# Early weight pieces kept in one line each, the last output tiles stored in four parts from two queues, and a new order of loads and due times, in an attention kernel with two expert layers

## The chip, the cores and the metric

The kernel runs on one core of a Trainium2 chip. The time is device microseconds of one execution. PE is the matrix engine, with PEld for its weight loads; DVE is the vector engine, ACT the scalar engine, POOL GpSimd, and SP the engine that only issues DMAs. 16 DMA engines move the data of all queues.

## What is computed

Four batches of eight heads pass through an attention over 32 memory slots; the result goes through a leaky expert layer with weights `w_in` and `w_out`, and then through four experts that are mixed by `domain_probs`. The weights of the first layer arrive as float64 and are rebuilt as float32 on the chip.

```python
a = softmax(phi, axis=2)                       # over 576 positions
k_m, v_m = a.T @ k, a.T @ v                    # 32 slots per head
attn = softmax(scale * q @ k_m.T) @ v_m
x = attn.transpose(0, 2, 1, 3).reshape(2304, 512)
h = x @ w_in;  x = maximum(0.01 * h, h) @ w_out
p = domain_probs / domain_probs.sum(-1)
for e in range(4):
    out += p[:, e:e+1] * (maximum(x @ w1[e], 0) @ w2[e])
```

## The kernel before, in words

Every float32 product is made of three products of rounded parts (a high and a low part of each operand). Work runs in three stages: the attention of batch 0 with the first weight pieces; the first expert layer (lines L960 and L1027 to L1029), with the attention of batches 1 to 3 and further weight pieces placed between; and the second layer (L1136 and L1204 to L1206) with its output stores.

A planner (`Plan`) collects operations with an engine, an estimated cost and a due time, and `issue` writes them out in the order of its own clock. `SHIFTS` changes the due times of ranges of operations. What each engine does is therefore a fixed row; each engine works through its row in order, and an instruction that waits holds everything behind it on that engine.

The loads of `phi`, `k`, `q` and `v` of each batch, the raw weight pieces and the stores are all issued by SP. Eight DMA semaphores are used in turn, so a DMA also waits for the one eight places ahead of it to land.

A raw weight piece (512 KB, 1,024 numbers of 4 bytes on each partition) lands in one of three buffers (`raws`) or, for the fourth to the seventh piece, in room that is still free in `xx`, which later holds the first layer's sum (`more0` to `more3`). `xx` has four lines of 2,304 numbers on each partition, a line being split in four stretches of 576, one for each batch; the same room holds `k`, `v` and `q` of the batches until they are used (`HOME`: batch 1's `v` in stretch 1 of all four lines, its `q` in stretch 2, its `k` in stretch 3). Before the change a `more` piece lies in 512 columns of one stretch of two neighbouring lines. The distance between its first and its last number then spans parts of all stretches of these lines. The waits that the framework puts in go by such spans: in the program before, steps on `more` pieces wait for batch 1's `v` load, which touches none of their numbers, and that load waits for steps on `more` pieces.

`piece64` rebuilds a piece in four steps on ACT, DVE and POOL (L858, L862, L870 or L868, L878); `split` then makes the two rounded parts (L341, L344). Each token tile of the second layer's last group ends in one DVE operation (L1223), after which SP stores 128 rows of 2 KB (L1235); stores of earlier groups (L1231) are made in four parts of 32 rows.

Of the kernel before, what the change touches and what calls it, by code (L numbers as in the profile page):

```python
# [15 lines left out]
ALU = mybir.AluOpType  # L16
# [4 lines left out]
SHIFTS = [  # L21
    (411, 34, 3.8), (30, 16, -39.9), (40, 2, -21.2), (265, 1, -16.9), (266, 2, -2.6), (440, 3, -3.1), (77, 12, -10.1)
]
# [13 lines left out]
class Plan:  # L37
# [6 lines left out]
    SPARE = 0.5  # L44
    NEAR = 0.1
    BANKS = 8

# [52 lines left out]
    def issue(self):  # L100
        ops = self.ops
# [14 lines left out]
        while issued < len(ops):  # L116
            now = events[0][0]
            while events and events[0][0] <= now:
                _, n, what = heappop(events)
# [9 lines left out]
            for e, queue in [(e, q) for q in (ready, spare) for e in names]:  # L129
                skipped = []  # L130
                while free[e] <= now and queue[e]:
                    item = heappop(queue[e])
                    n = item[1]
# [40 lines left out]
                    for m in after[n]:  # L174
                        late = self.TRANSFER if e == "SP" else 0.0 if e in ops[m][0] else self.LATENCY
                        there[m] = max(there[m], now + us + late)
                        left[m] -= 1
                        if not left[m]:
                            heappush(events, (there[m], m, None))
# [5 lines left out]
def kernel(  # L185
# [13 lines left out]
    nc = tc.nc  # L199
# [137 lines left out]
    def engine(e):  # L337
        return {"DVE": nc.vector, "POOL": nc.gpsimd}[e]
# [436 lines left out]
    def raw_piece(src, due, after, alone=False):  # L775
# [5 lines left out]
        if RAWS <= n < RAWS + MORE:  # L781

            x = n - RAWS
            t, rk = places["X"][:, 2 + x // 2, x % 2 * 2:x % 2 * 2 + 2, 0:512], f"more{x}"
            if len(src.shape) == 2:
                src = src.rearrange("p (a b) -> p a b", a=2)
        else:
# [54 lines left out]
    def piece64(kind, n, sl, src, due, key, after):  # L842
# [31 lines left out]
        def add(e, out):  # L874
            cuts = [(slice(i, i + 1),) for i in range(2)] if e == "DVE" and rk[0] == "m" else [()]
            for cut in cuts:
                cut = (every, *cut)
                engine(e).tensor_tensor(out=out[cut], in0=fu[cut], in1=low[cut], op=ALU.add)  # L878
        plan.op("DVE", 0.42, due, lambda: nc.vector.tensor_single_scalar(fu, fu, 3, op=ALU.logical_shift_left),
# [307 lines left out]
    def second_products(t, n):  # L1187
# [4 lines left out]
        for i in range(2 * TPB):  # L1192
# [34 lines left out]
            if u == E - 1:  # L1227
                def fn(tt=tt, a_=a_, dst=dst):
                    if dst is None:
# [3 lines left out]
                        return  # L1233
                    for i, n, at in runs_of(tt):
                        nc.sync.dma_start(out=rows_of(out, at, n), in_=dst[i:i + n * M])  # L1235
                plan.op("SP", 0.8, due, fn, [("out", tt)], [])
        freed["v2"] += 1

# [13 lines left out]
    for x in range(MORE):  # L1252
        plan.ops[loaded["q1" if x < 2 else "k1"]][3].update({plan.writer[f"more{x}"], *plan.readers[f"more{x}"]})
    for first, count, shift in SHIFTS:
# [33 lines left out]
```

## Time and profile before

| | us |
|---|---|
| median of 3 runs (lowest, highest) | 1167.89 (1167.64, 1168.8) |
| the profiled execution's own time | 1166.8 |
| its span, from the first to the last instruction | 1164.8 |
| PE busy in the span | 1127.9 |
| DVE, ACT, POOL busy | 680.5, 442.6, 101.1 |
| busy PE in the first 100 us | 79.91 |
| last DVE operation ends | 1148.78 |

The span is 2.0 us shorter than the execution's own time, and the profiled execution is 1.1 us below the median. PE is busy nearly without a break between the first 70 us and 1148 us; the stretches ahead of that and behind it are where an engine other than PE sets the time. In the views, a line number such as L1223 is a line of the kernel.

### The profile page before, as it was taken

To read this page: it belongs to the slowest core of one execution; us is meant where nothing else is said; L and a number is where in the kernel's file an instruction comes from. 1 tells how busy PE (TensorE), PEld (TensorE's weight loads), DVE (VectorE), ACT (ScalarE), POOL (GpSimd) and SP (SyncE) were. 2 spreads that over 40 slices of the span, in tenths; PEclk is the share of its full clock that TensorE was granted. 3 is DMA by queue.
4 is the path that set the end of the run, shared out by engine and by line. 5 is a ranking of instruction groups with operands and counts; after the bars stand their busy time and mean duration, and the time that the engine had idled before them with its cause. 6 is when DMAs were issued, how large, how long until landed. Compare 5 with 4: busy or idle time off the path is not lost.

```text
span 1164.8 us, 18127 instructions
## 1 busy us (share of the span) xinstructions
PE 1127.9 (97%) x7414; PEld 1020.6 (88%) x7414; DVE 680.5 (58%) x1276; ACT 442.6 (38%) x895; POOL 101.1 (9%) x103
## 2 busy tenths in 40 slices
PE   6799999999999999999999999999999999999994
PEld 4479999999999999898998999999999999999993
DVE  5796576733346787767677654454566634454641
ACT  4565567743435544333324223222224213222220
POOL 2341125500000000000000000000000000000000
PEclk9799999999999999999999999999999999999997
DMA  9564013310000377534444644444444634444201
GB/s 335 172 216 129 30 38 120 116 37 1 2 19 32 118 267 261 189 146 184 180 178 145 217 152 156 163 163 163 148 157 134 210 139 163 163 163 158 94 11 54
DMA packets 54013, 160.84 MB, mean 138 GB/s; under 512 B 5803, under 2 KB 22187, under 8 KB 47787
## 3 DMA queue, kind: packets, MB, share of 16 engines
q1 hardware_dynamic: 49323, 100.97, 24.7%
q0 software_dynamic: 4608, 58.72, 14.3%
q8 instruction: 58, 0.95, 0.3%
q14 instruction: 24, 0.20, 0.0%
HBM read 125.60 MB, written 34.08 MB: 137 GB/s over the span
## 4 chain that ended last, share of the span: by engine, by line
PE 92%; DMA 3%; DVE 2%; ACT 0%; POOL 0%; issue 0%; SPq 0%; POOLq 0%; ACTq 0%
PE psum L1136 30%; PE psum L1205 11%; PE psum L1206 11%; PE psum L1204 11%; PE psum L960 8%; PE psum L1027 6%; PE psum L1028 5%; PE psum L1029 5%; DMA exact<-in_moe_w_out_dram 2%; PE psum L976 1%; DMA exact<-in_q_dram 1%; DVE rounded L344 1%; DMA exact<-in_v_dram 0%; DVE exact L545 0%; PE psum L573 0%
## 5 line engine op out<-in xcount | busy, mean ns | idle before, releaser
L1145 DVE TENSOR_TENSOR exact<-psum,exact 128x384 f32<-128x384 f32 x336 | 184.0, 556 | 271.9 <-PE psum L1136 270.1
L1152 ACT ACTIVATE rounded<-exact 128x384 fp32r<-128x384 f32 x192 | 100.8, 525 | 283.5 <-DVE exact L1145 281.8
L344 DVE TENSOR_TENSOR rounded<-exact,rounded 128x288 fp32r<-128x288 f32 (+2 forms) x224 | 123.3, 565 | 105.6 <-ACT rounded L341 104.5
L1206 PE MATMUL psum<-late,rounded 128*128 128x512 f32 x384 | 150.7, 392 | 0.0
L1205 PE MATMUL psum<-late,rounded 128*128 128x512 f32 x384 | 150.5, 392 | 0.0
L1204 PE MATMUL psum<-late,rounded 128*128 128x512 f32 x384 | 149.3, 389 | 0.0
L1136 PE MATMUL psum<-rounded 128*128 128x384 f32 x768 | 143.4, 336 | 0.0
L1136 PEld LDWEIGHTS psum<-rounded 128*128 128x128 f32 x768 | 135.0, 188 | 2.4 <-DVE exact L1145 0.3
L960 PE MATMUL psum<-rounded 128*128 128x288 f32 x768 | 124.5, 299 | 2.3 <-DVE rounded L344 2.3
L341 ACT CAST rounded<-exact 128x288 fp32r<-128x288 f32 (+4 forms) x239 | 114.7, 500 | 17.4 <-DMA exact<-in_moe_w_dram 3.5
L1027 PE MATMUL psum<-rounded 128*128 128x288 f32 x384 | 116.0, 302 | 4.0 <-ACT rounded L341 4.0
L960 PEld LDWEIGHTS psum<-rounded 128*128 128x128 f32 x768 | 109.3, 189 | 8.6 <-issue 4.0
L1028 PE MATMUL psum<-rounded 128*128 128x288 f32 x384 | 113.6, 296 | 1.4 <-DVE rounded L344 1.4
L1029 PE MATMUL psum<-rounded 128*128 128x288 f32 x384 | 113.5, 296 | 0.0
L1136 PE MATMUL psum<-late,rounded 128*128 128x384 f32 x576 | 109.7, 336 | 0.0
L1156 DVE SCALAR_TENSOR_TENSOR rounded<-exact,rounded 128x384 fp32r<-128x384 f32 x192 | 98.7, 550 | 13.0 <-ACT rounded L1152 13.0
L1136 PEld LDWEIGHTS psum<-late,rounded 128*128 128x128 f32 x576 | 102.0, 188 | 3.8
L1015 ACT ACTIVATE exact<-psum 128x288 f32<-128x288 f32 x128 | 52.5, 410 | 123.3 <-PE psum L960 117.3
L1167 ACT COPY exact<-psum 128x384 f32<-128x384 f32 x48 | 23.1, 481 | 198.1 <-PE psum L1136 196.8
L1206 PEld LDWEIGHTS psum<-late,rounded 128*128 128x128 f32 x384 | 72.0, 188 | 15.1
L1205 PEld LDWEIGHTS psum<-late,rounded 128*128 128x128 f32 x384 | 72.0, 188 | 13.4
L1204 PEld LDWEIGHTS psum<-late,rounded 128*128 128x128 f32 x384 | 72.1, 188 | 13.2
(113 smaller groups left out, 1677.9 us busy)
## 6 DMA issues: line engine op xcount, KB each, us to landing
rounded<-kept POOLq DMA_DIRECT2D x22, 1792.0 KB, 7.7
exact<-in_moe_w_dram SPq DMA_DIRECT2D x64, 512.0 KB
kept<-rounded SPq DMA_DIRECT2D x10, 1792.0 KB
w<-kept POOLq DMA_DIRECT2D x10, 1792.0 KB, 7.8
kept<-w SPq DMA_DIRECT2D x6, 1792.0 KB
exact<-in_moe_w_in_dram SPq DMA_DIRECT2D x16, 512.0 KB
exact<-in_moe_w_out_dram SPq DMA_DIRECT2D x16, 512.0 KB
exact<-in_k_dram SPq DMA_DIRECT2D x4, 1152.0 KB
```

The costliest lines, as they stand in the source:

```text
L341: nc.scalar.copy(out, in_) if e == "ACT" else engine(e).tensor_copy(out, in_)
L344: engine(e).tensor_tensor(out=out, in0=in0, in1=in1, op=ALU.subtract)
L960: nc.tensor.matmul(ps, lhsT=l, rhs=r, start=start and n == 0, stop=stop and n == len(seq) - 1)
L1027: nc.tensor.matmul(po, lhsT=w2l[:, ds_], rhs=th, start=first, stop=False)
L1028: nc.tensor.matmul(po, lhsT=w2h[:, ds_], rhs=tl, start=False, stop=False)
L1029: nc.tensor.matmul(po, lhsT=w2h[:, ds_], rhs=th, start=False, stop=last)
L1136: nc.tensor.matmul(ps[k][0:TB], lhsT=l, rhs=r, start=(i == 0), stop=(i == 5))
L1145: plan.op("DVE", dve2(TB), at[k], lambda: nc.vector.tensor_tensor(out=o, in0=ps[k][0:TB], in1=other, op=ALU.add), [ps[k], ok, from_], [key])
L1152: plan.op("ACT", act2(TB), at[k], lambda: nc.scalar.activation(out=th, in_=src, func=AF.Relu), [key, *h_from[hs[c, i]]], [keys[0]])
L1204: nc.tensor.matmul(po[0:DM], lhsT=tl, rhs=w2h[:, c], start=(p == 0 and c == 0), stop=False)
L1205: nc.tensor.matmul(po[0:DM], lhsT=th, rhs=w2l[:, c], start=False, stop=False)
L1206: nc.tensor.matmul(po[0:DM], lhsT=th, rhs=w2h[:, c], start=False, stop=(p == NP2 - 1 and c == 1))
```

## The change

The three parts: `more` pieces of one line each, the last tiles' stores in parts of 32 rows (two from SP, two from ACT), and a new order (a constant `SETTLE` in the planner, which counts an operation that waits for a load as ready 2.5 us later, and new `SHIFTS`). DVE adds of a `more` piece are no longer cut in two.

```diff
 SHIFTS = [
-    (411, 34, 3.8), (30, 16, -39.9), (40, 2, -21.2), (265, 1, -16.9), ...
+    (553, 34, 1.0), (417, 30, 3.4), (490, 3, -13.8), (250, 28, -6.7), ...
 ]
...
+    SETTLE = 2.5
...
                         late = self.TRANSFER if e == "SP" else 0.0 if e in ops[m][0] else self.LATENCY
+                        late += self.SETTLE * (e not in ("SP", "X") and "SP" in ops[m][0])
...
             x = n - RAWS
-            t, rk = places["X"][:, 2 + x // 2, x % 2 * 2:x % 2 * 2 + 2, 0:512], f"more{x}"
-            if len(src.shape) == 2:
-                src = src.rearrange("p (a b) -> p a b", a=2)
+            t, rk = xx[:, x, 2 * S:2 * S + size], f"more{x}"
+            if len(src.shape) == 3:
+                t = t.rearrange("p (a b) -> p a b", a=src.shape[1])
...
         def add(e, out):
-            cuts = [(slice(i, i + 1),) for i in range(2)] if e == "DVE" and rk[0] == "m" else [()]
-            for cut in cuts:
-                cut = (every, *cut)
-                engine(e).tensor_tensor(out=out[cut], in0=fu[cut], in1=low[cut], op=ALU.add)
+            engine(e).tensor_tensor(out=out, in0=fu, in1=low, op=ALU.add)
...
-                    for i, n, at in runs_of(tt):
-                        nc.sync.dma_start(out=rows_of(out, at, n), in_=dst[i:i + n * M])
+                    for i in range(0, P // 2, M):
+                        nc.sync.dma_start(out=rows_of(out, tt * P + i)[0], in_=dst[i:i + M])
                 plan.op("SP", 0.8, due, fn, [("out", tt)], [])
+                if final:
+                    def fn(tt=tt, dst=dst):
+                        for i in range(P // 2, P, M):
+                            nc.scalar.dma_start(out=rows_of(out, tt * P + i)[0], in_=dst[i:i + M])
+                    plan.op("ACT", 0.8, due, fn, [("out", tt)], [])
...
     for x in range(MORE):
-        plan.ops[loaded["q1" if x < 2 else "k1"]][3].update({plan.writer[f"more{x}"], *plan.readers[f"more{x}"]})
+        for name in ("q1", "k1"):
+            plan.ops[loaded[name]][3].update({plan.writer[f"more{x}"], *plan.readers[f"more{x}"]})
```

SP's row from its eighth load on, before. `att<-in_q` is batch 2's `q`, `exact<-in_v` and `exact<-in_q` are batch 1's `v` and `q`; names in brackets are the engines, or the earlier DMAs (DMAHW), that a row waits for.

```order
L523 DMA att<-in_q_dram 128x4x576 [waits DMAHW4_49,DMAHW0_49,PE_49]
L160 DMA exact<-in_moe_w_in_dram 128x2x512 [waits DMAHW1_49]
L160 DMA exact<-in_moe_w_out_dram 128x2x512 [waits DMAHW2_49,Activation_49]
L160 DMA exact<-in_moe_w_out_dram 128x2x512 [waits DMAHW3_49]
L160 DMA exact<-in_moe_w_in_dram 128x2x512 [waits Pool_49]
L160 DMA exact<-in_moe_w_in_dram 128x2x512 [waits DMAHW5_49,Pool_49]
L160 DMA exact<-in_moe_w_out_dram 128x1024 [waits DMAHW6_49,Pool_49]
L518 DMA att<-in_phi_dram 128x4x288 [waits DMAHW7_49]
L523 DMA exact<-in_v_dram 128x4x576 [waits PE_49,DMAHW0_49,Activation_49,Pool_49]
```

The same place of SP's row now:

```order
L162 DMA exact<-in_moe_w_in_dram 128x2x512 [waits DMAHW0_49]
L162 DMA exact<-in_moe_w_out_dram 128x1024 [waits DMAHW1_49]
L162 DMA exact<-in_moe_w_out_dram 128x1024 [waits DMAHW2_49]
L162 DMA exact<-in_moe_w_in_dram 128x2x512 [waits DMAHW3_49,Activation_49,Pool_49]
L162 DMA exact<-in_moe_w_in_dram 128x2x512 [waits DMAHW4_49,Pool_49]
L521 DMA att<-in_phi_dram 128x4x288 [waits DMAHW5_49]
L162 DMA exact<-in_moe_w_out_dram 128x1024 [waits DMAHW6_49,Pool_49]
L526 DMA exact<-in_v_dram 128x4x576 [waits PE_49,DMAHW7_49,Activation_49,Pool_49]
L526 DMA att<-in_q_dram 128x4x576 [waits DMAHW0_49]
```

Batch 2's `q` has moved behind batch 1's `v`, so three `more` pieces no longer stand behind a wait for PE; batch 1's `v` keeps its waits for ACT and POOL.

DVE's row before, around the steps L870 on `more` pieces. Of the four DMA semaphores of the first of these, DMAHW0 is batch 1's `v` load; that of the third, DMAHW2, is batch 1's `q` load. The row before the first is the low part of the first layer's projected weights, which PE waits for.

```order
L344 TENSOR_TENSOR rounded<-psum,rounded 128x512 [waits PE_49]
L870 SCALAR_TENSOR_TENSOR exact<-exact 128x2x256 [waits DMAHW2_49,DMAHW1_49,DMAHW7_49,DMAHW0_49,Activation_49]
L870 SCALAR_TENSOR_TENSOR exact<-exact 128x2x256 [waits DMAHW3_49,DMAHW1_49]
L703 TENSOR_TENSOR att<-att 128x18x32
L344 TENSOR_TENSOR rounded<-exact,rounded 128x288 [waits Activation_49]
L879 TENSOR_SCALAR exact<-exact 128x512
L708 TENSOR_REDUCE att<-att 128x18 [waits Activation_49]
L710 RECIPROCAL att<-att 128x18 [waits DVE_49]
L714 TENSOR_TENSOR att<-att 128x18x32 [waits DVE_49]
L717 STREAM_TRANSPOSE exact<-att 128x576 [waits DVE_49]
L870 SCALAR_TENSOR_TENSOR exact<-exact 128x2x256 [waits DMAHW2_49]
```

The same steps now (L873); DMAHW7 of the first is batch 1's `v` load, and DMAHW2 of the last is that `more` piece's own load.

```order
L347 TENSOR_TENSOR rounded<-att,rounded 128x2x288 [waits Activation_49]
L873 SCALAR_TENSOR_TENSOR exact<-exact 128x512 [waits DMAHW7_49,DMAHW0_49]
L873 SCALAR_TENSOR_TENSOR exact<-exact 128x512 [waits DMAHW1_49]
L347 TENSOR_TENSOR rounded<-psum,rounded 128x512 [waits PE_49]
L697 STREAM_TRANSPOSE att<-psum 128x2x5x32 [waits Pool_49]
L697 STREAM_TRANSPOSE att<-psum 128x2x4x32 [waits DVE_49]
L704 TENSOR_REDUCE att<-att 128x18 [waits DVE_49]
L706 TENSOR_TENSOR att<-att 128x18x32 [waits DVE_49]
L879 TENSOR_SCALAR exact<-exact 128x512
L873 SCALAR_TENSOR_TENSOR exact<-exact 128x512 [waits DMAHW2_49]
```

One wait for batch 1's `v` is left, now ahead of the projected weights' low part; the wait for batch 1's `q` is gone.

SP's row at the end of the program, before: one store, or two where a tile crosses a half batch, for each of the last six tiles.

```order
L1235 DMA out_dram<-exact 4x32x512
L1235 DMA out_dram<-exact 2x32x512 x2
L1235 DMA out_dram<-exact 4x32x512
L1235 DMA out_dram<-exact 3x32x512
L1235 DMA out_dram<-exact 32x512
L1235 DMA out_dram<-exact 4x32x512 x2
```

The ends of SP's and of ACT's rows now:

```order
L1235 DMA out_dram<-exact 32x512 x12
L1240 DMA out_dram<-exact 32x512 x12
```

Eight stores became 24 of 64 KB, half of them on ACT, which has nothing else left there.

## Rows read from the trace of the kernel before

**Rows 1.** The page: busy time by engine, and the chain that ended last.

```profile
PE 1127.9 (97%) x7414; PEld 1020.6 (88%) x7414; DVE 680.5 (58%) x1276; ACT 442.6 (38%) x895; POOL 101.1 (9%) x103
...
PE 92%; DMA 3%; DVE 2%; ACT 0%; POOL 0%; issue 0%; SPq 0%; POOLq 0%; ACTq 0%
```

**Rows 2.** Windows: length, busy time of PE, PEld, DVE, ACT, POOL, clock, DMA share, GB/s.

```profile
0.00:100.00 100.00, 79.91 (x904) 61.69 (x905) 74.85 (x122) 58.66 (x110) 36.31 (x36) 0.91 0.61 213
...
33.50:66.60 33.10, 22.81 (x270) 17.57 (x268) 24.62 (x31) 19.03 (x32) 14.94 (x10) 0.84 0.54 182
...
66.60:1148.00 1081.40, 1081.14 (x6836) 989.33 (x6836) 634.74 (x1204) 407.80 (x840) 77.56 (x76) 1.00 0.38 132
...
1130.00:1165.00 35.00, 17.99 (x82) 14.80 (x80) 8.09 (x14) 1.58 (x3) 0.00 (x0) 0.79 0.15 46
```

**Rows 3.** Timeline of PE: start, length, instruction, idle before and its releaser.

```profile
66.60 0.38 PE L616 MATMUL psum<-att,exact 128*128 128x2 f32 x2 [1.39 <-DVE rounded L344]
```

**Rows 4.** The chain that ended last, 20 to 62 us: start, length, what.

```profile
32.76 5.41 DMA exact<-in_v_dram
...
42.48 6.74 DMA exact<-in_q_dram
```

**Rows 5.** Waits from 25 to 40 us: who waited for what, total, times, longest.

```profile
ACT exact L858 <- DMA exact<-in_v_dram: 5.5, 1, 5.5
```

**Rows 6.** Timeline of DVE, 30 to 56 us.

```profile
32.81 0.68 DVE L344 TENSOR_TENSOR rounded<-psum,rounded 128x512 fp32r<-128x512 f32 x1
38.25 1.30 DVE L870 SCALAR_TENSOR_TENSOR exact<-exact 128x512 uint32<-128x512 uint32 x2 [4.76 <-issue]
...
41.23 1.54 DVE L344 TENSOR_TENSOR rounded<-exact,rounded 128x288 fp32r<-128x288 f32 x1
...
49.24 0.69 DVE L870 SCALAR_TENSOR_TENSOR exact<-exact 128x512 uint32<-128x512 uint32 x1 [2.47 <-DMA exact<-in_q_dram]
```

**Rows 7.** Timeline of SP's DMA issues, 0 to 60 us.

```profile
7.06 0.55 SPq L160 DMA_DIRECT2D exact<-in_moe_w_in_dram  x1
17.25 0.37 SPq L523 DMA_DIRECT2D att<-in_q_dram  x1
...
32.76 0.37 SPq L523 DMA_DIRECT2D exact<-in_v_dram  x1
...
42.48 0.37 SPq L523 DMA_DIRECT2D exact<-in_q_dram  x1
```

**Rows 8.** Timelines of PE and of POOL, 12 to 62 us.

```profile
17.15 4.16 PE L593 MATMUL psum<-exact,att 64*128 64x256 f32 x36
...
32.00 2.45 PE L478 MATMUL psum<-att 128*128 128x512 f32 x3
...
28.07 1.30 POOL L878 TENSOR_TENSOR w<-w,exact 128x512 uint32<-128x512 uint32 x1 [2.67 <-ACT exact L868]
```

**Rows 9.** Timeline of DVE, from 1147 us to the end.

```profile
1148.03 0.75 DVE L1223 SCALAR_TENSOR_TENSOR exact<-psum,exact 128x512 f32<-128x512 f32 x1 [0.61 <-PE psum L1206]
```

**Rows 10.** Windows of the end of the program, columns as in rows 2.

```profile
1143.00:1148.80 5.80, 4.99 (x23) 3.79 (x21) 3.34 (x5) 0.00 (x0) 0.00 (x0) 1.00 0.24 59
1148.80:1154.00 5.20, 0.00 (x0) 0.00 (x0) 0.00 (x0) 0.00 (x0) 0.00 (x0) 0.63 0.37 102
1154.00:1159.00 5.00, 0.00 (x0) 0.00 (x0) 0.00 (x0) 0.00 (x0) 0.00 (x0) 0.50 0.26 90
...
1163.00:1165.00 2.00, 0.00 (x0) 0.00 (x0) 0.00 (x0) 0.00 (x0) 0.00 (x0) 0.50 0.02 7
```

**Rows 11.** Timelines of SP: eight early 64 KB stores, and the last eight.

```profile
895.28 3.76 SPq L1231 DMA_DIRECT2D out_dram<-exact  x8
...
1142.01 11.14 SPq L1235 DMA_DIRECT2D out_dram<-exact  x8
```

**Rows 12.** Windows behind the first issue and behind the last of the eight early stores.

```profile
896.00:896.50 0.50, 0.50 (x5) 0.50 (x4) 0.50 (x1) 0.00 (x0) 0.00 (x0) 1.00 0.61 123
...
900.00:900.50 0.50, 0.50 (x4) 0.42 (x3) 0.29 (x1) 0.00 (x0) 0.00 (x0) 1.00 0.00 0
```

More of the change, by code (lines that the diff above doesn't have):

```diff
@@ L21 @@
 SHIFTS = [
-    (411, 34, 3.8), (30, 16, -39.9), (40, 2, -21.2), (265, 1, -16.9), (266, 2, -2.6), (440, 3, -3.1), (77, 12, -10.1)
+    (553, 34, 1.0), (417, 30, 3.4), (490, 3, -13.8), (250, 28, -6.7), (643, 12, -17.4), (245, 9, -18.3),
+    (528, 3, -41.5), (100, 1, -9.4), (318, 30, 112.8), (316, 28, -7.4), (601, 12, -7.9),
 ]
```

## The prediction, written before the changed kernel was run

> **What bounds the kernel now.** I read the page first, then windows, then what waits where. On the page PE is busy 1127.9 of 1164.8 us, and the chain that ended last is 92% PE and only 3% DMA [rows 1]. The windows show where the other time lies [rows 2]. From 66.6 to 1148 us PE is busy 1081.14 of 1081.40 us at full clock, so no order of loads can gain anything there. In the first 100 us PE is busy 79.91, so about 20 us are idle; in the last 35 us it is busy 17.99. The last real wait of PE in the front is the 1.39 us before L616 of batch 1, at 66.60 us [rows 3]; I use this matmul as the mark. The time is therefore the moment of the mark, plus a fixed row of PE work, plus what lies behind the last matmul. The change touches the first and the third of these and must be priced in both.
>
> **The tail.** The last DVE operation ends at 1148.78 [rows 9], the span at 1164.8. For 16.0 us nothing but stores runs. They are not held back by the amount of data: in the two stretches in which most of it moves, the DMA share is 0.37 and 0.26, against 0.24 while the last tiles are still being made [rows 10]. A share of about a quarter is about 4 of the 16 engines, and the last stores are 4x32x512, four parts outermost. The kernel already has stores of the other shape: eight stores of 64 KB with 32 rows outermost at 895.28. Their issue takes SP 3.76 us for eight, 0.47 each [rows 11]; 0.72 us after the first issue the share is 0.61, about 10 engines, and by 900.0 us, 0.96 us after the last issue ended, it is 0.00 again [rows 12].
>
> The change gives the last tile four such stores, two from SP and two from ACT, so each engine issues two. From the last DVE operation on: start 0.05, the second issue 0.47 later, 0.72 until its data moves, 0.5 for the data, and 1.5 to close, which I take from the old end, where the share has fallen to 0.02 in the last 2 us [rows 10]. That is 3.2 us in place of 16.0, a gain of 12.8. This is the short end; it supposes that both issuers work side by side and that earlier stores are out of the way. The long end: all 24 stores pass one issue path, 24 x 0.47 = 11.3 us from the old first issue at 1142.01 [rows 11], so to 1153.3; with 0.72 + 0.5 + 1.0 behind it the end is at 1155.5, 6.7 us after the last DVE operation, a gain of 9.3. I take 4.0 us, nearer the short end, because the early stores show eight issues in 3.76 us from SP alone, and the tiles are finished over more time than twelve issues of one engine (5.6 us) need. **Tail gain 12.0, bounds 9.3 to 12.8.** ACT has no work there any more (0.00 busy from 1143 us on [rows 10]), so the new DMAs on it hold up nothing.
>
> The row on the share of 0.26 agrees with the Trainium skill, "DMA: Bandwidth & Descriptors", section "Why a DMA increments its semaphore by 16 and not by 1": the number of engines is the largest number up to 16 that divides the outermost sizes, which is 4 for 4x32x512 and 16 for 32x512. The same page speaks against the change under "Rules for kernel authors": below 64 KB a transfer is mostly overhead, and small ones should be joined; and its section "Issuing engines are not separate DMA queues" says that a second issuer saves only issue time. Taken alone, these would keep the tail near its old length; how much of that I allow is rival C below.
>
> **The front: which waits go.** In the program before, batch 1's `v` load is issued at 32.76 and takes 5.41 us on the chain, and batch 1's `q` load at 42.48 takes 6.74 [rows 4, 7]. Both stand on the chain although what waits for them doesn't read their data: ACT's L858 on a `more` piece is held 5.5 us by the `v` load [rows 5], and DVE is idle 4.76 us before its first L870 and 2.47 us before its third, the latter put down to the `q` load [rows 6]. On DVE these are 4.76 + 2.47 = 7.2 us. Behind the first of them stand DVE's steps for batch 1, for which PE waits at the mark through L344 [rows 3].
>
> With a piece in one line, the span of a piece no longer meets the `q` room, and that wait is gone from the row of DVE. The wait for `v` is not: `v` fills all four lines, and the first L873 on a `more` piece still waits for it. What is late next is this load. Its row on SP now stands behind the waits for ACT and POOL, where before it also stood behind batch 2's `q`, `p1` and the rest of the row: SP issued one weight piece at 7.06 and the next row, batch 2's `q`, only at 17.25, when PE let it [rows 7]. Two of the things that the load waits for can be placed: the product of batch 0's `v` ends at 17.15 + 4.16 = 21.31, and the POOL add of an early piece ended at 28.07 + 1.30 = 29.4 in the old order [rows 8]. With the weight pieces no longer behind `q`, I put that add and so the issue at 28, the landing at 28 + 5.4 = 33.4 and DVE's arrival at 31 (it ended its L344 of 32.81 at 33.5 [rows 6], and its row now has a little less ahead). About 2 us of the 7.2 remain: 5.2 saved. To that comes PE's own row: by the two orders it has done 36 L960 products at the mark in place of 30, work that then need not be done later. At PE's steady pace, 1081.14 us for 6836 matmuls or 0.158 each [rows 2], six are 0.9; they stand where PE would wait, so I count them whole and round. **Front gain 6.0.**
>
> Bounds: the lower one is 0, if another wait takes the place of this one at once. PE is busy 22.81 of 33.10 us between 33.5 and 66.6, at a clock of 0.84, and DVE 24.62 [rows 2]; PE waits for DVE, DVE for ACT and both for loads by turns there, so a saved microsecond is easily lost. The upper one by DVE is 33.10 - 24.62 = 8.5 us, all its idle time in the stretch, plus 0.9: 9.4. Above that, only both loads whole, 5.41 + 6.74 = 12.15, are a limit [rows 4]. I hold to 6.0 because DVE's row is the one that must run down before the mark, and the two waits are counted in it.
>
> **Edits at nothing.** The add of a `more` piece in one instruction in place of two saves a start on DVE or nothing; the one-line read does not change the number of elements. A DVE step that shares its time with POOL could stretch when more of them meet: the L344 of 41.23 took 1.54 us [rows 6]; two such steps, 3.1 us, lie within the lower bound. `SETTLE` only moves rows. PE's row has three more idle matmuls (L478) ahead of the mark, 12 for 9; a group of three took 2.45 us [rows 8]. They are put where PE waits; where it doesn't wait any more they cost up to that, which is inside the bound of 0. `k1` and `q1` now wait for all four pieces; the work that hides them is the first layer's, between the mark and their use, and if that cover were gone it would cost one more load of 5 to 7 us [rows 4].
>
> **Sum.** Profiled execution 1166.8 - 12.0 - 6.0 = 1148.8. It lies 1.1 below the median of the runs, so the time to forecast is 1149.9, about 1150.
>
> **Rivals.**
> A. *The front gives nothing.* The end of the `v` wait is replaced by a wait for weight pieces or for PE's own chain through batch 1. For it: PE's clock of 0.84 and the idle time of every engine in the stretch [rows 2]; ACT's L858 sat as long behind the `v` load as DVE did [rows 5]. Against it: two named idle times on the one engine that PE waits for. Time: 1149.9 + 6.0 = 1155.9.
> B. *Both loads leave the chain whole.* 12.15 in place of 6.0: 1143.7. It needs the `v` load to be issued some 5 us earlier than I think. Against it: the POOL add at 28.07 [rows 8].
> C. *The tail is issue-bound.* The 24 small stores pass one path, or ACT's half starts late; the gain is 9.3 or less: 1152.6 with my front, later if the overhead of small stores is worse. Against it: eight of them at 0.47 [rows 11].
> D. *Slower.* The new row on SP holds batch 1's `v` ahead of `q2`, `q1` and `k1`. If its waits for ACT and POOL end late, all three queue behind it, each a load of 5.4 to 6.7 us [rows 4], and batch 1's whole chain moves. It decides from the point where the mark comes 12 us later than at 66.60, at 78.6: then the tail's gain is eaten. At two such loads, 12.1, the time is 1167.9 - 12.0 + 12.1 = 1168, and at three 1174. For it: SP already stood from 7.06 to 17.25 behind one such row [rows 7]. Against it: PE's product of `v` ends at 21.31 and POOL's add near 29 [rows 8], before the old issue of 32.76.
>
> **How the numbers follow.** Forecast 0.58 (its own range 1146 to 1155.6), A 0.22, B 0.09, C 0.08, D 0.03. About 0.2%, 2.3 us, is what a measurement of this kernel can tell from no change. Faster by more than that are the forecast, A, B and C, less the edge of C in which the tail gives nothing and the front nothing: 0.95. Within it 0.02, slower 0.03. The range leaves out half of B, the late part of A and C, and D: 1145 to 1157.5.
>
> **What would show it.** Tail: after the last DVE operation 3 to 7 us to the end of the span, and a share above 0.5 while the last stores move. If the share stays near 0.25, the shape was not the cause. Front: the mark (L616 of batch 1) at about 60.6 in place of 66.60, no wait of DVE on batch 1's `q`, one of at most about 2 us on its `v`, and that load issued before 30 us. If DVE's waits are gone and the mark has not moved, rival A holds; if the mark is later than 66.60, D. The forecast is wrong if PE between the mark and its last matmul is no longer busy without a break.

## The result, and the profile after

The changed kernel takes 1151.37 us (median of four runs, 1149.29 to 1152.57) against 1168.3 us before (median of four as well; the forecast started from 1167.89, the median of three of these four). The ratio is 0.9854 with a 95% interval of 0.9836 to 0.9871: 17.1 us faster, between 15.1 and 19.2. The forecast was 1150, its range 1145 to 1157.5. The profiled execution took 1151.32 us, with a span of 1149.5.

First the page: busy time by engine, and the chain that ended last. They answer to [rows 1].

```profile
PE 1127.0 (98%) x7420; PEld 1020.6 (89%) x7420; DVE 676.2 (59%) x1279; ACT 440.5 (38%) x893; POOL 98.2 (9%) x102
...
PE 95%; DMA 2%; DVE 2%; issue 0%; SPq 0%; ACT 0%; POOL 0%; DVEq 0%
```

PE does the same work, 1127.0 us busy, in a span that is 15.3 us shorter. Where these 15.3 us lie is told by two moments, the mark (L619 of batch 1, L616 before) and the last DVE operation. The timelines of PE and of DVE of the changed kernel, as [rows 3] and [rows 9]:

```profile
59.85 0.38 PE L619 MATMUL psum<-att,exact 128*128 128x2 f32 x2
...
1145.13 0.75 DVE L1223 SCALAR_TENSOR_TENSOR exact<-psum,exact 128x512 f32<-128x512 f32 x1 [0.61 <-PE psum L1206]
```

The mark came at 59.85 in place of 66.60, 6.75 us earlier. The last DVE operation ends at 1145.88 in place of 1148.78, only 2.90 us earlier. And from there to the end of the span it is 3.6 us in place of 16.0: 12.4 us. So 2.9 + 12.4 = 15.3, and 3.85 us of what the front had gained were given back between the mark and the end.

The tail in windows (length, busy PE, PEld, DVE, ACT, POOL, clock, DMA share, GB/s), against [rows 10]:

```profile
1143.00:1145.88 2.88, 2.09 (x10) 1.40 (x8) 1.66 (x3) 0.00 (x0) 0.00 (x0) 1.00 0.71 202
1145.88:1147.50 1.62, 0.00 (x0) 0.00 (x0) 0.00 (x0) 0.00 (x0) 0.00 (x0) 1.00 0.74 195
1147.50:1149.50 2.00, 0.00 (x0) 0.00 (x0) 0.00 (x0) 0.00 (x0) 0.00 (x0) 1.00 0.12 41
```

and the timelines of SP and ACT, against [rows 11]:

```profile
1139.11 7.58 SPq L1235 DMA_DIRECT2D out_dram<-exact  x12
...
1139.11 7.64 ACTq L1240 DMA_DIRECT2D out_dram<-exact  x12
```

The share while the last stores move is 0.74 where it was 0.26 to 0.37, and both issuers are done 0.9 us after the last DVE operation.

The front: what PE and DVE still wait for. Timelines of PE and DVE, against [rows 6]:

```profile
36.94 1.30 PE L960 MATMUL psum<-rounded 128*128 128x288 f32 x4 [7.23 <-DVE rounded L347]
...
34.90 1.29 DVE L873 SCALAR_TENSOR_TENSOR exact<-exact 128x512 uint32<-128x512 uint32 x2 [4.56 <-DMA exact<-in_v_dram]
```

and the piece of the chain that is the load of batch 1's `v`, against [rows 4]:

```profile
27.41 7.39 DMA exact<-in_v_dram
```

DVE no longer waits for batch 1's `q`. It still waits 4.56 us for `v`, which was issued 5.35 us earlier than before but took 7.39 us in place of 5.41. PE's longest idle time, 7.23 us, ends with the DVE step behind this one. Windows from the start to the mark, of the kernel before and of the changed one:

```profile
0.00:66.60 66.60, 46.71 (x578) 31.30 (x578) 45.05 (x71) 34.81 (x56) 23.58 (x27) 0.87 0.73 258
```

```profile
0.00:59.85 59.85, 44.16 (x591) 30.43 (x591) 41.68 (x76) 32.88 (x55) 21.82 (x26) 0.94 0.77 279
```

Of the 6.75 us, 4.20 are idle time of PE that is gone (19.89 to 15.69) and 2.55 are busy time: PE did a little more work in less time, since its granted clock was 0.94 in place of 0.87.

Between the mark and the end, the timeline of PE has this:

```profile
61.08 0.29 PE L1028 MATMUL psum<-rounded 128*128 128x288 f32 x1
63.73 0.30 PE L1029 MATMUL psum<-rounded 128*128 128x288 f32 x1 [2.35 <-issue]
```

and the windows, from the mark to the last DVE operation and of 3.4 us that begin 1 us behind that stall:

```profile
59.85:1145.88 1086.03, 1082.79 (x6834) 990.13 (x6830) 634.56 (x1204) 407.60 (x838) 76.35 (x76) 1.00 0.38 132
...
64.75:68.15 3.40, 3.40 (x21) 3.07 (x18) 2.84 (x4) 0.79 (x2) 1.34 (x2) 0.50 1.04 398
```

PE stood 2.35 us in the middle of three products of one bank, with "issue" as the cause: no semaphore that the profile shows. In the 3.4 us of the second window the granted clock was 0.50, the lower of the two levels, 1.2 and 2.4 GHz. From the mark to the last DVE operation it was 1086.03 us, 1082.79 of them busy; before, the same stretch was 1148.78 - 66.60 = 1082.18, with 1081.14 busy [rows 2]. So 2.2 us more idle and 1.65 us more busy make the 3.85 us. The idle part is the stall; 3.4 us at half the clock cost 1.7 us, which is about the busy part.

### The profile page after: what moved, and what is told of

The parts are those of the page before. It is cut to its first block, busy times and chain, and to the rows that moved or that the text cites. A ratio compares the mean times of both kernels' runs of the same rounds, so it can differ in the third digit from the quotient of the medians.

```text
span 1149.5 us, 18174 instructions
## 1 busy us (share of the span) xinstructions
PE 1127.0 (98%) x7420; PEld 1020.6 (89%) x7420; DVE 676.2 (59%) x1279; ACT 440.5 (38%) x893; POOL 98.2 (9%) x102
## 4 chain that ended last, share of the span: by engine, by line
PE 95%; DMA 2%; DVE 2%; issue 0%; SPq 0%; ACT 0%; POOL 0%; DVEq 0%
PE psum L1136 31%; PE psum L1206 12%; PE psum L1205 12%; PE psum L1204 11%; PE psum L960 9%; PE psum L1027 6%; PE psum L1029 6%; PE psum L1028 6%; PE psum L976 1%; DMA exact<-in_moe_w_out_dram 1%; DMA exact<-in_v_dram 1%; PE psum L576 1%; PE psum L607 1%; PE psum L685 0%; DVE exact L873 0%
## 5 line engine op out<-in xcount | busy, mean ns | idle before, releaser
L347 DVE TENSOR_TENSOR rounded<-exact,rounded 128x288 fp32r<-128x288 f32 (+3 forms) x223 | 123.5, 569 | 102.7 <-ACT rounded L344 101.9
L344 ACT CAST rounded<-exact 128x288 fp32r<-128x288 f32 (+2 forms) x240 | 115.2, 500 | 14.1 <-DVE exact L820 3.9
L1206 PEld LDWEIGHTS psum<-late,rounded 128*128 128x128 f32 x384 | 72.0, 188 | 15.1
```

Of the source, the lines that this page charges most:

```text
L344: nc.scalar.copy(out, in_) if e == "ACT" else engine(e).tensor_copy(out, in_)
L347: engine(e).tensor_tensor(out=out, in0=in0, in1=in1, op=ALU.subtract)
L1206: nc.tensor.matmul(po[0:DM], lhsT=th, rhs=w2h[:, c], start=False, stop=(p == NP2 - 1 and c == 1))
```

## The experiments

All ratios are against the kernel before, run on the same chip in turn with the experiment; its medians there were 1167.71, 1168.02 and 1167.98 us. Gains are given with the 95% interval of the ratio.

**The tail alone, two issuers.** The kernel before with only this edit:

```diff
-                    for i, n, at in runs_of(tt):
-                        nc.sync.dma_start(out=rows_of(out, at, n), in_=dst[i:i + n * M])
+                    for i in range(0, P // 2, M):
+                        nc.sync.dma_start(out=rows_of(out, tt * P + i)[0], in_=dst[i:i + M])
...
+                        for i in range(P // 2, P, M):
+                            nc.scalar.dma_start(out=rows_of(out, tt * P + i)[0], in_=dst[i:i + M])
```

> The kernel before with the new stores of the last tiles alone. Theory (the shape of the stores is the whole tail): in the two profiles the time from the last DVE operation to the end of the span went from 16.0 to 3.6 us, so this run gains 12.4 us, 1155.9 us against 1168.3, with the front as before (L616 of batch 1 near 66.6 us). Rival (small stores pay an overhead, part of the gain came from the new order): a gain under 10 us, and more than 6 us from the last DVE operation to the end.

Measured: 1154.59 us, ratio 0.9891 (0.9878 to 0.9905), a gain of 12.7 us (11.1 to 14.2). Windows from the last DVE operation (1149.16) on:

```profile
1149.16:1151.00 1.84, 0.00 (x0) 0.00 (x0) 0.00 (x0) 0.00 (x0) 0.00 (x0) 1.00 0.74 211
1151.00:1153.00 2.00, 0.00 (x0) 0.00 (x0) 0.00 (x0) 0.00 (x0) 0.00 (x0) 0.53 0.04 11
```

From there to the end it is 3.84 us, near the 3.6 of the changed kernel. The stores alone give the whole tail, and the new order has no part in it.

**The tail alone, all four parts from SP.**

```diff
-                    for i, n, at in runs_of(tt):
-                        nc.sync.dma_start(out=rows_of(out, at, n), in_=dst[i:i + n * M])
+                    for i in range(0, P, M):
+                        nc.sync.dma_start(out=rows_of(out, tt * P + i)[0], in_=dst[i:i + M])
```

> As the run before, but all four parts of each tile are issued by SP. Theory (the shape counts, the second queue only saves issue time): the last tile needs two more issues of SP, 2 x 0.47 = 0.9 us, so about 1156.8 us. Rival (two issuers are needed): 24 issues in a row from the first at 1142.0 end at 1153.3, and the span 2.2 us later; the gain is 9.3 us, 1159 us.

Measured: 1157.99 us, ratio 0.9923 (0.9909 to 0.9936), a gain of 9.0 us (7.5 to 10.6). Timelines of SP and of DVE:

```profile
1142.68 11.49 SPq L1235 DMA_DIRECT2D out_dram<-exact  x24
...
1148.71 0.75 DVE L1223 SCALAR_TENSOR_TENSOR exact<-psum,exact 128x512 f32<-128x512 f32 x1 [0.61 <-PE psum L1206]
```

The time lies between the two expectations, but the rows speak for the rival: 24 issues take 11.49 us, 0.48 each, and end at 1154.17, 4.7 us behind the last DVE operation; the span ends 2.5 us later, at 1156.7. The tail is 7.2 us. Of the 12.7 us about 9 come from the new parts and 3.7 from the second issuer.

The new parts are both smaller and of another shape, and no run took the two apart. A large store with many rows outermost stands in the kernel before: L830 stores 1,792 KB with 128 rows outermost in one DMA, issued at 405.01. In a window of that store (kernel before) the share is 0.95, so the size of the old last stores is not what held them at 0.26 to 0.37:

```profile
407.00:410.00 3.00, 3.00 (x18) 2.73 (x17) 2.99 (x8) 1.87 (x6) 0.00 (x0) 1.00 0.95 401
```

**The front alone.** The changed kernel with the old stores of the last tiles (the first edit, undone there).

> The changed kernel with the old stores of the last tiles. Theory (the two halves add up, and 3.85 us of the front's 6.75 us are lost again behind the mark by a stall of PE): 1151.4 + 12.4 = 1163.8 us, L619 of batch 1 near 59.9 us, and PE idle again for about 2.3 us near 61 us. Rival (that stall was an accident of one execution): no such idle time, and 1160 us.

Measured: 1164.94 us, ratio 0.9966 (0.9953 to 0.9978), a gain of 4.0 us (2.6 to 5.5). With the tail's 12.7 that is 16.7, which is what the whole change gives (17.1) within the intervals. The mark is at 59.92, and PE's timeline has the stall again, before the same matmul:

```profile
63.91 0.40 PE L1029 MATMUL psum<-rounded 128*128 128x288 f32 x1 [2.45 <-issue]
```

So it is no accident of one execution. The eight runs lie in two groups, three at 1161.0 to 1161.6 with a mean granted clock of 0.991 to 0.992, and five at 1164.8 to 1165.6 with 0.986 to 0.990. Only one of the five was profiled, so what the three were spared stays open.

**The layout alone.** The kernel before with pieces in one line, and the loads of `q` and `k` behind the steps on all of them:

```diff
-            t, rk = places["X"][:, 2 + x // 2, x % 2 * 2:x % 2 * 2 + 2, 0:512], f"more{x}"
+            t, rk = xx[:, x, 2 * S:2 * S + size], f"more{x}"
...
-            cuts = [(slice(i, i + 1),) for i in range(2)] if e == "DVE" and rk[0] == "m" else [()]
+            engine(e).tensor_tensor(out=out, in0=fu, in1=low, op=ALU.add)
...
-        plan.ops[loaded["q1" if x < 2 else "k1"]][3].update({plan.writer[f"more{x}"], *plan.readers[f"more{x}"]})
+        for name in ("q1", "k1"):
+            plan.ops[loaded[name]][3].update({plan.writer[f"more{x}"], *plan.readers[f"more{x}"]})
```

> The kernel before with the one-line layout of the early pieces, the uncut adds and the waits of q1 and k1 that go with it; the old order and the old stores. Theory (the layout removes the wait for q of batch 1, 2.47 us on DVE, and leaves that for v, 4.76 us, which the new order treats): a gain between 0 and 2.5 us, 1166 to 1168 us, DVE still idle 4 to 5 us behind the v load. Rival (the layout is what gives the front): about 1162 to 1164 us.

Measured: 1167.55 us, ratio 0.9998 (0.9989 to 1.0007): nothing. DVE still stands 4.80 us before the first step on an early piece, and PE waits for what comes behind it (timelines of DVE and PE):

```profile
36.81 1.29 DVE L870 SCALAR_TENSOR_TENSOR exact<-exact 128x512 uint32<-128x512 uint32 x2 [4.80 <-issue]
...
41.37 0.61 PE L1025 MATMUL psum<-rounded 128*128 128x288 f32 x1 [5.97 <-DVE rounded L344]
...
62.58 0.38 PE L616 MATMUL psum<-att,exact 128*128 128x2 f32 x2 [3.18 <-DVE exact L545]
```

The wait for `q` is gone from DVE's row, and the kernel is not faster by it. L616 comes 4.0 us earlier than before, but it stands at another place of PE's row here, with 436 products ahead of it in place of 578, so that is no gain.

**The order alone.** The kernel before with the new `SHIFTS` and `SETTLE`, old layout, old stores.

> The kernel before with the new order alone (SHIFTS and SETTLE); old layout of the early pieces, old stores of the last tiles. The layout alone gave nothing (1167.55 against 1167.71), layout and order together 2.8 us. Theory (they need each other): the old layout puts the waits for v and q of batch 1 back on DVE, and the new order alone gives nothing or loses, 1167 to 1170 us. Rival (the order is the whole front): 1161 to 1165 us.

Measured: 1164.87 us, ratio 0.9972 (0.9961 to 0.9983), a gain of 3.3 us (2.0 to 4.6). My theory that order and layout need each other fell: the order alone gives as much as both together (4.0, 2.6 to 5.5). DVE's only wait for a load there is one of 3.01 us for `v`; none for `q` is left, though the layout is the old one:

```profile
35.97 1.29 DVE L873 SCALAR_TENSOR_TENSOR exact<-exact 128x512 uint32<-128x512 uint32 x2 [3.01 <-DMA exact<-in_v_dram]
```

**The wait for `v` taken away.** The changed kernel, with the load of `v` put behind the steps on the three pieces whose span it meets:

```diff
+    for x in range(3):
+        plan.ops[loaded["v1"]][3].update({plan.writer[f"more{x}"], *plan.readers[f"more{x}"]})
     plan.issue()
```

> The changed kernel with the load of batch 1's v put behind the steps on the first three early pieces, so that no step of DVE waits for it any more. Theory (that wait, 4.56 us on DVE, is what PE's longest idle time, 7.23 us before L960 at 36.94 us, hangs on): the idle time falls by 4 to 5 us, 1147 us, or 1151 if what is gained is lost in the stall near 61 us. Rival (weight pieces or the chain of batch 1 take its place): the idle time moves to another row and the time stays within 1 us of 1151.4.

Measured: 1144.24 us, ratio 0.9795 (0.9783 to 0.9808), 7.1 us below the changed kernel and 23.9 below the kernel before. Timelines of DVE, PE and SP:

```profile
30.28 1.29 DVE L873 SCALAR_TENSOR_TENSOR exact<-exact 128x512 uint32<-128x512 uint32 x2
...
32.31 0.97 PE L960 MATMUL psum<-rounded 128*128 128x288 f32 x4 [2.40 <-DVE rounded L347]
...
34.00 0.38 SPq L526 DMA_DIRECT2D exact<-in_v_dram  x1
```

The step runs at 30.28 in place of 34.90, PE's idle time is 2.40 in place of 7.23, and the load, issued 6.6 us later, is waited for by nobody. The wait that was left in the changed kernel was a wait for data that nobody needed yet. The gain is more than the theory's: the mark comes at 56.39, 3.5 us earlier, and from there to the last DVE operation it is 1082.36 us, 3.7 less than in the changed kernel, since the stall behind the mark is down to 0.36 us and the granted clock of that stretch is 1.00. So about half of the 7.1 us comes from the stall.

**The same in the kernel before.** Old layout, old order, old stores; only `v`, `q` and `k` of batch 1 put behind all steps on the early pieces:

```diff
+    for x in range(MORE):
+        for name in ("v1", "q1", "k1"):
+            plan.ops[loaded[name]][3].update({plan.writer[f"more{x}"], *plan.readers[f"more{x}"]})
     plan.issue()
```

> The kernel before, in its old layout, old order and old stores, with one edit: the loads of v, q and k of batch 1 are put behind all steps on the early pieces. Theory (the waits of DVE for loads that it doesn't read, 4.76 and 2.47 us, bound the front of the kernel before): 4 to 7 us less, 1161 to 1164 us. Rival (weight pieces, the clock and batch 1's own chain would have taken the place of these waits): within 1.5 us of 1168.

Measured: 1160.48 us, ratio 0.9937 (0.9923 to 0.9950), a gain of 7.4 us (5.8 to 9.0). Timelines of DVE and of PE:

```profile
33.56 1.28 DVE L870 SCALAR_TENSOR_TENSOR exact<-exact 128x512 uint32<-128x512 uint32 x2
...
42.04 0.65 DVE L870 SCALAR_TENSOR_TENSOR exact<-exact 128x512 uint32<-128x512 uint32 x1
...
60.38 0.39 PE L616 MATMUL psum<-att,exact 128*128 128x2 f32 x2 [1.07 <-DVE rounded L344]
```

Both waits of DVE that the prediction named are gone: the steps run at 33.56 and 42.04 in place of 38.25 and 49.24. The mark comes 6.2 us earlier, and from it to the last DVE operation it is 1082.21 us, as before (1082.18): nothing is given back. PE's idle time ahead of the mark fell by 4.1 us, its busy time by 2.1 at a granted clock of 0.92 for 0.87. That the whole gain is near the 7.2 us of the two waits is therefore partly chance. These three lines give more than the change's whole front.

**The old layout under the new order, with the loads late.** The changed kernel with the old lines of the layout and the edit above.

> The changed kernel with the old layout of the early pieces, and the loads of v, q and k of batch 1 put behind all steps on them, so that no step waits for a load that it doesn't read. Theory (the layout counts for nothing by itself; what counts is which loads DVE waits for): 1144 to 1146 us. Rival (the layout is needed, since the loads of batch 1 now come later and PE waits for them): 1148 us or more.

Measured: 1148.99 us, ratio 0.9837 (0.9824 to 0.9850): the rival's time, 4.8 us above the run with the new layout. Its reason does not hold: from 20 to 62 us no engine waits for `v`, `q` or `k`. Of its waits from 15 to 50 us (who waited for what, total, times, longest) this one is ACT's:

```profile
ACT w L861 <- DMA exact<-in_moe_w_out_dram: 3.0, 2, 2.8
```

A window of this kernel, and below it the same of the kernel with the new layout and `v` late:

```profile
20.00:34.90 14.90, 11.52 (x106) 5.30 (x102) 11.66 (x23) 10.64 (x20) 5.10 (x4) 0.77 0.81 294
```

```profile
20.00:34.90 14.90, 11.22 (x127) 5.60 (x124) 13.93 (x27) 12.02 (x23) 6.93 (x5) 0.93 0.77 288
```

In this stretch DVE does 2.3 us less work in the old layout, ACT is held 2.8 us by a raw piece, and PE's granted clock is 0.77 for 0.93. The same wait of ACT, 2.8 us long, stands in the run with the order alone, which has the old layout too, and neither in the changed kernel nor in the run with `v` late, so it goes with the layout. So the layout is worth something once the wait for `v` is out of the way, and nothing that I can resolve before. How much is not quite settled: `v` waits for the fourth piece as well here and is issued at 41.17 in place of 34.00. Which of the spans brings the wait for that piece was not tried.

**`SETTLE` at 0** in the changed kernel.

> The changed kernel with SETTLE at 0 and everything else as it is. Theory (SETTLE only moves rows; the step on the early piece waits for v on DVE as before): 1150 to 1153 us. Rival (counting waits for loads as longer is what keeps steps from standing in front of late data): 1154 us or more, with a new wait of DVE or ACT for a load.

Measured: 1151.18 us, ratio 0.9856 (0.9843 to 0.9870): no difference from 1151.37. The wait for `v` stands in it as before, 3.37 us. Behind the mark (59.98) the rows differ: PE's stall is 1.35 us, no stretch at the lower clock follows it, and PE waits 1.28, 0.93 and 0.75 us more between 88 and 108 us. So a stall does not bring the lower clock every time; that it did in the changed kernel is not shown.

**PE's stall: the loads held.** The changed kernel with `phi`, `v`, `v` and `k` of batches 2 and 3 made to wait for the DVE operation that reads the mark's product:

```diff
+    zs = [n for n, o in enumerate(plan.ops) if getattr(o[2], "__code__", None) and o[2].__code__.co_firstlineno == 622]
+    for name in ("p2", "v2", "v3", "k2"):
+        plan.ops[loaded[name]][3].add(zs[1])
```

> The changed kernel with the loads of batches 2 and 3 (phi, two v, k), which filled all DMA engines from 57.5 us on, held until DVE has read the result of L619. Theory (PE's 2.35 us at 61.4 us before L1029, with no semaphore wait, are a late fetch of its program behind these loads; the instruction queue moves 16 KB at 61.35 us, just as PE runs dry): the idle time is gone and with it the half clock behind it, 3.7 us, 1147.7 us. Rival (the stall belongs to the instruction, or loads that come later make PE wait elsewhere): 1151 us or more, and an idle time of over 2 us before L1029.

Measured: 1148.43 us, ratio 0.9833 (0.9820 to 0.9846), 2.9 us below the changed kernel. The four runs spread from 1146.51 to 1151.00, and the interval meets that of the changed kernel (0.9836 to 0.9871), so the times alone do not quite settle the gain. PE's timeline:

```profile
60.45 0.29 PE L1029 MATMUL psum<-rounded 128*128 128x288 f32 x1 [0.79 <-issue]
```

and the DMA queues from 58.2 to 59.2 us (packets, MB, share of 16 engines):

```profile
q1 hardware_dynamic: 63, 0.06, 16.9%
q8 instruction: 1, 0.02, 5.5%
```

The stall before the same matmul is 0.79 in place of 2.35 us. The instruction queue q8 moves one 16 KB block there. Its count fits PE's program: 58 blocks in the whole span for some 14,840 matmuls and weight loads, one for every 256, and 59 for 15,080 in the next run. The block begins at 58.23 and ends at 59.11, and PE goes on 1.34 us after that. In the changed kernel the DMA queues from 61.3 to 62.4 us, just as PE stands, show that same block among data that fill the engines:

```profile
q1 hardware_dynamic: 153, 0.32, 85.2%
q8 instruction: 1, 0.02, 5.7%
```

It moves from 61.35 to 62.34, and PE goes on 1.39 us later. The theory is half right: the stall is shorter, not gone. A part of this run's gain is another thing: in its profile the load of `v` took 5.73 us in place of 7.39, though the program up to there is the same. The mark comes 1.7 us earlier by that; from the mark to the last DVE operation it is 1082.93 us in place of 1086.03, and these 3.1 us are what the held loads gave in this profile.

```profile
27.37 5.73 DMA exact<-in_v_dram
```

**PE's stall: the block's edge moved.**

```diff
+        for _ in range(5):
+            nc.tensor.matmul(psum[:, bank, 0:2], lhsT=ident, rhs=ident[:, 0:2], start=True, stop=True)
```

These lines stand behind the idle matmul, so 60 tiny matmuls are added. In the trace each of them is two, with two weight loads (7,540 matmuls for 7,420), so PE's row grows by 240 instructions, twice what the expectation below counts.

> The changed kernel with 60 tiny matmuls (2 columns) more, five behind each of the twelve idle matmuls, which stand where PE waits. Only the place of PE's instructions within the 16 KB blocks of its program moves, by some 120 instructions. Theory (late fetch at a block's edge): L1029 near 61 us no longer waits; an idle time without a wait, if there is any, stands some 60 matmuls earlier in PE's row or falls into a wait that is there anyway: 1147.5 to 1151.5 us. Rival (the wait belongs to that matmul): PE idle 2.3 us before the same L1029, 1151.4 us or more.

Measured: 1156.27 us, ratio 0.9900 (0.9884 to 0.9916). The time is a miss: the tiny matmuls were not free, PE is busy 93.36 of the first 100 us for 81.97. But the place is clear. Timeline of PE:

```profile
71.52 0.65 PE L664 MATMUL psum<-att,exact 128*64 128x128 f32 x4
73.85 0.32 PE L664 MATMUL psum<-att,exact 128*64 128x128 f32 x1 [1.68 <-issue]
```

The three products before which PE stood are done without a stop, and it stands in the middle of a run of L664, again with no releaser. The block of PE's program moves from 71.49 to 72.54; PE goes on 1.31 us later. So the stall belongs to the block of the program, not to the matmul. A count of PE's instructions in the traces (matmuls, weight loads and its sequencer's) says the same: in the nine other profiles with this stall PE stops when 1,217 or 1,218 of them have begun, whatever the order, and here when 1,474 have, one block of 256 later.

**Both edits.** The changed kernel with `v` late and the later loads held.

> The changed kernel with both edits: batch 1's v load behind the steps on the first three early pieces, and the loads of batches 2 and 3 held until L619 of batch 1 has been read. Theory (each edit takes away a wait of its own, but with the first one PE's stall at a block's edge was only 0.36 us long): 1143 to 1144.5 us against 1144.24 with the first alone. Rival (the held loads are worth the 2.9 us that they gave alone): 1141 us.

Measured: 1143.42 us, ratio 0.9790 (0.9777 to 0.9803). As the theory said, 0.8 us below the run with `v` late alone, which the intervals do not tell apart. It has the lowest median of this study, 24.5 us (23.0 to 26.0) below the kernel before.

## Why the prediction was right

**The bound.** PE is as busy as before, and the time moved with the front and the tail, as the prediction read it. What it said would make it wrong, a break in PE's work between the mark and the end, did come.

**The tail: right, 12.4 us in the profile and 12.7 alone, for 12.0.** The end lies 3.6 us behind the last DVE operation; I took 4.0. The reason also held, shape before amount: the share rose from 0.26 to 0.74, and a large store with 128 rows outermost runs at 0.95. What I left to a bound, that all 24 issues pass one path, is real with one issuer: SP alone leaves 7.2 us, near the 6.7 that I gave for the long end (there I took 1.0 us to close, at the short end 1.5; with 1.5 it is 7.2). The second issuer is worth 3.7 us, not a remainder. Against that, the rule of the Trainium skill in "DMA: Bandwidth & Descriptors", "Rules for kernel authors", that transfers under 64 KB are mostly overhead, did not bear here: stores of 64 KB, just at that bound, beat the larger ones by 9 to 13 us, at a share of 0.74 for 0.26 to 0.37. What the Trainium skill says in the same page under "Issuing engines are not separate DMA queues", that a second one only saves issue time, agrees; at the end of a program that is 3.7 us.

**The mark: right, 59.85 for 60.6.** The wait for `q` was gone, and the load of `v` was issued at 27.41, for 28 in the prediction. The reason given for the former does not hold: a piece of one line fills stretch 2 of its line and most of stretch 3 (`xx[:, x, 2 * S:2 * S + size]`), so it lies in the room of `q`. No step waits for `q` any more because its load now comes behind the steps on all four pieces; with the old layout that wait goes as well, by the new order alone or by the loads put late. The rest of that step was mis-sized: I took 5.4 us for the load, from the row of before, and so 2 us for DVE's remaining wait; the load took 7.39 in the profile (7.66 and 5.73 in two others of the same order) and the wait was 4.56. That the mark came out right all the same is partly luck: the prediction counted 7.2 - 2 + 0.9 where DVE's waits fell by 7.2 - 4.56 = 2.7, and the 0.9, for six products done ahead of the mark, shortens the row behind the mark and cannot move the mark itself. The rest of the 6.75 comes from order and clock, which it did not price: 2.55 us of it are busy time at a higher granted clock. Two readings of rows were off without weight in the sum: `p1`, batch 1's `phi`, still stands ahead of `v` in the new row of SP, and the 2.45 us for a group of three idle matmuls are the end of a group of six records that took 5.17 us, two records being one idle matmul.

**The step that failed: the row of PE work behind the mark is not fixed.** The prediction took the mark's gain, 6.0, for the front's gain. 3.85 us of 6.75 were given back behind it: a stall of 2.35 us at a block of PE's program, and 1.65 us more of busy time, with a stretch at half the clock in it. The run with `v` late (1082.36 us behind the mark, in place of 1086.03) and the kernel before with its loads late (1082.21) show that a gain at the mark goes through where no such stall stands. The front's net gain is 2.9 us in the profile and 4.0 (2.6 to 5.5) alone. In the sum 2 us too much for the front stood against 0.7 too little for the tail, and the forecast lies 1.4 us below the measured median.

**The wrong credit within the front.** The prediction gave the lost wait for `q`, and with it a third of DVE's 7.2 us, to the layout. Layout alone gave 0.2 us (-0.8 to 1.3), order alone 3.3, both 4.0. That the two waits bound the front was right, and shown in the kernel before itself: with the loads behind the steps it is 7.4 us faster.

**The rivals.** A (the front gives nothing) did not come about, though half of its mechanism did: another wait, behind the mark, took 3.85 of the 6.75 us. B (both loads leave the chain) comes out in the run with `v` late, 1144.24 us for the 1143.7 that B gave, but by another way: B asked for an earlier issue of `v`, and there it is issued later. C is the run with SP alone. D did not show: the load of `v` was issued before the old time. `SETTLE` moved the time by nothing, as said.

## What to carry to other kernels

A wait that is put in by address span rather than by data costs what a real one costs: look for engines that wait for a load whose bytes they never read, and move the load behind the step instead of hurrying it; here one edit of that kind gave 7.4 us, and on top of the change 7.1, half of which was a stall of PE that went with it. At the end of a program nothing hides a store: give the last ones a shape that spreads over more DMA engines (a share of 0.74 for 0.26 to 0.37 here), and issue them from two engines. A gain at a mark in the middle is a gain of the time only if everything behind it is bound by work: compare the stretch behind the mark in both traces before you add it up.

## What the runs showed of the hardware

In these traces PE stops at the edge of a block of its program when the block comes late. In ten of the fourteen profiles of this study a PE idle time of 0.35 to 2.45 us ends 1.31 to 1.53 us after the last byte of a 16 KB block on the instruction queue, a block that moves somewhere from 56 to 73 us; in the other four (the kernel before among them) no idle time over 0.25 us ends there. The Trainium skill, "Runtime: NRT & Kernel Launch", section "Instruction fetch mechanics", calls the crossing of such a boundary mostly hidden; in the front of this kernel it was not. How long the stall is follows from two times, both counted from the moment when PE begins the block ahead (1,217 less 256, so 961 in the count above; 57.95 us in the changed kernel). All in us:

| | block landed after | PE done with the 256 after | landed + 1.4 - done | stall |
|---|---|---|---|---|
| changed kernel | 4.39 | 3.43 | 2.4 | 2.35 |
| loads held | 2.87 | 3.43 | 0.8 | 0.79 |
| `v` late | 4.33 | 5.40 | 0.3 | 0.36 |
| both | 2.51 | 5.40 | none | none |

In the other ten profiles the same sum comes within 0.15 us of the stall. With the loads held that otherwise fill the DMA engines the block lands 1.5 to 1.8 us sooner, in both pairs of profiles. With `v` late it lands as late as in the changed kernel, among loads at the same share (1.05; a packet counts whole where it begins, so a share can pass 1), but PE takes 2 us longer over the block ahead:

```profile
56.70:57.70 1.00, 1.00 (x9) 1.00 (x9) 0.53 (x3) 0.97 (x4) 1.00 (x1) 1.00 1.05 403
```

How far ahead PE asks for a block, and why the transfer of a block began 3.4 us after PE had begun the one ahead with the engines full and 1.3 to 2.0 us with the loads held, the traces do not tell.

The second thing is the load of `v`: in the same place of the same order it took 5.73, 7.39 and 7.66 us in three executions. In the two slow ones 15 of its 16 shares had landed 5.4 us after the issue and the last one 2 us later, and a step that waits for the load pays for the last.
